# Two token tiles per numerator step in a fused linear-attention and token-mixing kernel

## The chip, the cores and the metric

The kernel runs on one core of a Trainium2 chip, as one launch. The metric is the device time of a launch in microseconds. Five engines run side by side, each through its own list of instructions, in order: TensorE (PE, with its weight loads PEld), VectorE (DVE), ScalarE (ACT), GpSimd (POOL) and SyncE (SP), which here only issues transfers. Semaphores order them where one needs another's result or buffer.

## The reference

Shapes: x 2048 x 512, 32 heads of 16, w1 2048 x 1792, w2 1792 x 2048. All fp32.

```python
q, k, v = split_heads(layernorm(x) @ wqkv)
pq, pk = per_head(q, w_phi), per_head(k, w_phi)
phi_q = concat([softmax(pq), softmax(-pq)])       # over the 16 features, per head
phi_k = concat([softmax(pk), softmax(-pk)])
kv, z = phi_k.T @ v, phi_k.sum(tokens)            # per head
num = phi_q @ kv
den = phi_q @ z + 1e-6
h   = x + (num / den) @ wo
u   = gelu(einsum("sd,sf->df", layernorm(h), w1) + b1)   # across tokens
out = h + (u @ w2 + b2).T
```

## The kernel before

The 2048 tokens are 16 tiles of 128. A matmul of fp32 values is made from three (L62 to L64, `mm3`): operands are split in a high and a low part (`xs`, `whi`/`wlo`, `oh`/`ol`, `hs`) and high x high, low x high, high x low are summed in PSUM.

The launch goes through these stages. Weights are folded and K and V are projected for all tiles, to 113 us; q tiles 0 to 5 are projected among them. A bridge (L419 to L508, to 143.7 us) finishes K and V, makes `zacc` (the sum of phi_k over tokens), spreads it over partitions with a matmul of ones (L487, copied to `zB` at L488), copies wo (`woh`, `wol`) and starts q tiles 6 to 9. The token loop (L630 to L667, 143.7 to 271.5 us) has 19 iterations and is a pipeline over token tiles. The rest of the first matmul of the token mixing runs to 387 us, and the second (`py`, L761) to the end.

From L419 to L669 the orders of PE, DVE, ACT and POOL are written by hand: an instruction stands on its engine where its Python call stands. Only SP's order is a planner's. What an iteration `it` of the loop does, by the names used below:

- q tile: `q_mm` projects a q tile (12 matmuls of 512 columns) into `pu`, a PSUM pool of two buffers. `logit_ops` (L134 to L154) gives DVE three steps per tile: maximum `mx` (L152) and minimum `mn` (L153) per head, and the shift (L145) that writes v-mx into the first half of `eq`. For tiles 0 to 5 the negative logits mn-v are DVE's as well (L150). For tiles 6 to 15 ACT copies v out of PSUM into the second half of `eq` (L147), and later POOL's `negate` (L160) makes mn-v of it in place. `q_exp` (L171, ACT) takes the exponential of both halves; `q_sums` (L216, DVE) sums it per head, once for each half.
- denominator: `ez` (L442, POOL) multiplies by zB, `s_den` (L451 to L457, DVE) sums and divides to a weight `w` for each head and half, and `s_pq` (L460, POOL) scales `eq` by it.
- `s_tr(it)`: PE transposes `eq` in 8 blocks into the PSUM tile `tn` (L525), ACT copies it to `pht` (L527, two copies).
- `s_num(it-1)`: the numerator, 32 small matmuls of 64 rows x 32 columns in the array and 128 tokens (L543), four of a row's blocks and two rows side by side; it uses `tn` too, of which there is one buffer of two banks. ACT copies it to `oh` (L547) and DVE forms `ol` (L552).
- `s_wo(it-2)`: 12 matmuls with wo to `po`; `s_h` (L568, DVE) adds x and stores h. `s_moments`, `s_rstd` and `s_hn` (ACT, POOL) make the layernorm of h and split it to `hs` (L57, L58).
- fills: from iteration 4 (LAG) on, `fill(p)` adds one h tile to the first token-mixing product for a pair p of 128-column blocks of w1 (6 matmuls); p=0 uses the pool `ps_f`, and p=1 `ps_q` once q's tiles are through. `fill_load` loads a w1 part (two token tiles at once), ACT makes `whi` (L604), and `flush` puts the DVE subtraction `wlo` (L596) where it is called.

In iterations 0 to 4 the q tiles 10 to 15 are projected: tile 10 in iteration 0, 11 and 12 in iteration 1, then one in each.

## Time and profile before

| what | us |
|---|---|
| time, median of 3 (lowest, highest) | 534.8 (534.78, 535.04) |
| the profiled execution, its own time | 535.27 |
| its span in the profile | 533.5 |
| token loop, start of first transposes | 143.70 |
| PE busy in 165 to 200 | 32.72 of 35.00 |
| PE busy in 200 to 271.5 | 71.50 of 71.50 |
| PE busy in 271.5 to 387 | 115.50 of 115.50 |
| PE busy in 387 to 533.5 | 141.09 of 146.50 |

The granted clock of TensorE is 0.999. A row of instructions names line, engine, operation, output and inputs, partitions x elements, and how many; then busy time in us, the mean of one in ns, and the idle time of the engine just before them with what ended it. A row of the timeline has start and duration in us first, and in brackets the engine's idle time before it and its releaser. Matmuls overlap: one of 512 columns lasts 390 ns or so but the next starts 227 ns after it.

### The profile page before, as it was taken

Reading aid. Unit: us, or ns where it says so; the run is one execution under the profiler, and the core shown is the slowest. Engines: PE = TensorE matmul, PEld = TensorE weight load, DVE = VectorE, ACT = ScalarE, POOL = GpSimd, SP = SyncE. Lnnn points to the kernel's source line nnn. Section 1 sums busy time; section 2 is a strip of 40 time slices with the busy share of each in tenths; the row PEclk is TensorE's granted clock in tenths of the full one; section 3 lists DMA queues with packets and bytes.
Section 4 is the critical chain, followed back from the end, with each engine's and each line's share of the span. In section 5 each row is a group of like instructions: output and inputs, shape, how many; then the busy total and the mean of one; then the engine's idle time right before and its main releaser. Section 6 shows DMA issues by size and latency. Waiting matters only on the chain.

```text
span 533.5 us, 9887 instructions
## 1 busy us (share of the span) xinstructions
PE 523.4 (98%) x3872; PEld 451.0 (85%) x3872; DVE 382.5 (72%) x680; ACT 277.6 (52%) x470; POOL 228.3 (43%) x180
## 2 busy tenths in 40 slices
PE   8999999999999899999999999999999999999995
PEld 7888888887877777778788888888899999999995
DVE  6893999878798979784235523835768878887784
ACT  6998833525447777666766423525443343343340
POOL 2589699877876978985345000000001101100110
PEclk9999999999999999999999999999999999999999
DMA  8544310022302223333355333533014556535631
GB/s 303 196 124 119 86 35 21 1 62 78 101 1 83 95 81 119 120 109 111 95 159 182 99 100 99 159 111 87 20 41 110 138 149 146 131 120 120 158 78 43
DMA packets 45487, 55.85 MB, mean 105 GB/s; under 512 B 3968, under 2 KB 33024, under 8 KB 45440
## 3 DMA queue, kind: packets, MB, share of 16 engines
q1 hardware_dynamic: 43136, 51.38, 30.3%
q0 software_dynamic: 2016, 3.67, 5.1%
q8 instruction: 30, 0.49, 0.4%
q10 hardware_dynamic: 288, 0.17, 0.1%
q14 instruction: 17, 0.14, 0.1%
HBM read 46.81 MB, written 8.39 MB: 103 GB/s over the span
## 4 chain that ended last, share of the span: by engine, by line
PE 90%; DVE 5%; ACT 3%; issue 1%; POOL 1%; DVEq 0%; ACTq 0%; POOLq 0%
PE py L761 26%; PE pu L62 12%; PE pu L64 12%; PE pu L63 11%; PE po L62 3%; PE pv L63 2%; PE tn L525 2%; PE pv L64 2%; PE pv L62 2%; PE pk_ps L62 2%; PE po L63 2%; PE po L64 2%; PE pk_ps L64 2%; PE pk_ps L63 2%; PE tn L543 2%; PE kvp L207 1%
## 5 line engine op out<-in xcount | busy, mean ns | idle before, releaser
L799 POOL DMA_DIRECT2D out<-ot x14 | 12.5, 1001 | 212.1 <-DVE ot L797 212.1
L761 PE MATMUL py<-uf,whi 128*128 128x256 f32 x560 | 96.2, 283 | 0.0
L62 PE MATMUL pu<-hs,whi 128*128 128x512 f32 x224 | 87.6, 394 | 0.7 <-ACT eq L147 0.7
L57 ACT ACTIVATE whi<-wraw 128x1792 fp32r<-128x1792 f32 x28 | 47.7, 1705 | 77.9 <-PE py L761 62.9
L63 PE MATMUL pu<-hs,whi 128*128 128x512 f32 x224 | 87.2, 389 | 0.0
L64 PE MATMUL pu<-hs,wlo 128*128 128x512 f32 x224 | 87.0, 390 | 0.2 <-DVE wlo L596 0.2
L761 PEld LDWEIGHTS py<-uf,whi 128*128 128x128 f32 x560 | 83.3, 192 | 0.0
L596 DVE TENSOR_TENSOR wlo<-wraw,whi 128x512 fp32r<-128x512 f32 x56 | 46.3, 841 | 45.2 <-ACT whi L604 44.0
L761 PE MATMUL py<-uf,wlo 128*128 128x256 f32 x280 | 69.9, 283 | 0.0
L58 DVE TENSOR_TENSOR wlo<-wraw,whi 128x1792 fp32r<-128x1792 f32 x28 | 56.6, 2023 | 17.8 <-ACT whi L57 17.8
L604 ACT ACTIVATE whi<-wraw 128x512 fp32r<-128x512 f32 x56 | 34.4, 627 | 45.6 <-PE pu L63 41.6
L62 PEld LDWEIGHTS pu<-hs,whi 128*128 128x128 f32 x224 | 42.1, 188 | 9.3 <-ACT eq L147 1.2
L64 PEld LDWEIGHTS pu<-hs,wlo 128*128 128x128 f32 x224 | 42.1, 188 | 9.3 <-DVE wlo L596 0.6
L761 PEld LDWEIGHTS py<-uf,wlo 128*128 128x128 f32 x280 | 49.7, 192 | 0.0
L63 PEld LDWEIGHTS pu<-hs,whi 128*128 128x128 f32 x224 | 42.1, 188 | 8.4
L442 POOL TENSOR_TENSOR ez<-eq,zB 128x1024 f32<-128x1024 f32 x16 | 39.5, 2474 | 0.1
L761 PE MATMUL py<-un,whi 128*128 128x256 f32 x224 | 38.4, 283 | 0.0
L195 POOL TENSOR_TENSOR pk<-pk,sk 128x1024 f32<-128x1024 f32 x16 | 31.1, 1944 | 9.8 <-DVE sk L194 9.0
L460 POOL TENSOR_TENSOR eq<-eq,w 128x1024 f32<-128x1024 f32 x16 | 31.0, 1940 | 5.9 <-DVE w L457 5.9
L527 ACT ACTIVATE pht<-tn 128x512 f32<-128x512 f32 x32 | 17.4, 596 | 30.8 <-PE tn L525 30.8
L761 PEld LDWEIGHTS py<-un,whi 128*128 128x128 f32 x224 | 33.2, 192 | 0.1
L199 POOL TENSOR_TENSOR zacc<-zacc,pk 128x1024 f32<-128x1024 f32 x13 | 31.3, 2406 | 0.6
(165 smaller groups left out, 1192.8 us busy)
## 6 DMA issues: line engine op xcount, KB each, us to landing
wraw<-in_w SPq DMA_DIRECT2D x112, 256.0 KB, 2.9
xraw<-in_xT SPq DMA_DIRECT2D x16, 256.0 KB, 3.1
xh<-in_x SPq DMA_DIRECT2D x16, 256.0 KB, 2.6
h<-in_x SPq DMA_DIRECT2D x16, 256.0 KB, 3.1
out<-h SPq DMA_DIRECT2D x16, 256.0 KB, 2.0
out<-ot POOLq DMA_DIRECT2D x14, 256.0 KB, 4.6
wraw<-in_wT SPq DMA_DIRECT2D x12, 256.0 KB, 5.0
wo<-in_wo SPq DMA_DIRECT2D x4, 256.0 KB, 4.7
```

The costliest lines, as they stand in the source:

```text
L57: nc.scalar.activation(hi, src, AF.Copy)
L58: lo_engine.tensor_sub(lo, src, hi)
L62: nc.tensor.matmul(o, ah, bh, start=first, stop=False)
L63: nc.tensor.matmul(o, ah, bl, start=False, stop=False)
L64: nc.tensor.matmul(o, al, bh, start=False, stop=last)
L195: nc.gpsimd.tensor_mul(heads(PK[t]), heads(PK[t]), sk.unsqueeze(2).to_broadcast([P, 2 * H, DH]))
L199: nc.gpsimd.tensor_add(zacc, zacc, PK[t])
L442: nc.gpsimd.tensor_mul(EZ[t], EQ[t], zB)
L460: nc.gpsimd.tensor_mul(heads(EQ[t]), heads(EQ[t]), W[t].rearrange("p g c h -> p (g c h)").unsqueeze(2).to_broadcast([P, 2 * H, DH]))
L596: LO.append(nc.vector.tensor_sub(wl_, raw, wh_).ins)
L604: nc.scalar.activation(wh_, raw, AF.Copy)
L761: nc.tensor.matmul(o, a[x], b[:, y], start=start and i == 0, stop=stop and i == 2, skip_group_check=True)
```

## The change

- The numerator goes by pairs of token tiles. `pht` holds two tiles, one buffer for all; `s_num(j)` works on tiles 2j and 2j+1 with 32 matmuls of 256 columns, in even iterations only. `oh` and `ol` hold a pair each, one buffer, and are still made tile by tile. `s_wo` and `s_h` stay one tile an iteration, two behind.
- The loop's body is in a new order. The scaling of tile it+1 (`s_pq`) comes first. In even iterations the numerator follows, then the layernorm of h tile it-4 and DVE's `ol`. Then ez, negate, the q tile, the fills, the exponential; after them wo and transposes (transposes first in odd iterations). DVE's logits, sums and denominators come next, then `flush`, then `s_h`.
- The first pair's fills start at iteration 5 and the second's at 6, one of each an iteration, with loads up to one part further ahead. When the loop ends, two and three fills of the pairs are left, for one of each before.
- q's negative logits, tiles 6 to 15: POOL computes mn-mx in place (32 numbers a partition), then subtracts the shifted half of `eq` from it. ACT's copy of v into the second half is still issued, now at the head of `logit_ops` ahead of mx and mn; negate overwrites its result without reading it.

In the changed program, for tiles 6 to 15, DVE's maximum carries a wait for ACT's copy of the same PSUM tile; before, ACT's copy carried a wait for DVE's shift. Ahead of the loop PE's order is the same in both. Counts of instructions are the same but for the numerator (256 small matmuls for 512) and POOL's ten small subtractions.

```diff
-LAG = 4
+LAG = 5
@@ logit_ops
+        if pool:
+            nc.scalar.activation(ev[:, :, 1], v, AF.Copy)
         def shift():
             nc.vector.tensor_sub(ev[:, :, 0], v, mx.unsqueeze(3).to_broadcast([P, NPR, 2, DH]))
             if pool:
-                nc.scalar.activation(ev[:, :, 1], v, AF.Copy)
-                MN.append((ev, mn))
+                MN.append((ev, mx, mn))
@@ negate
-            ev, mn = MN.pop(0)
-            nc.gpsimd.tensor_sub(ev[:, :, 1], mn.unsqueeze(3).to_broadcast([P, NPR, 2, DH]), ev[:, :, 1])
+            ev, mx, mn = MN.pop(0)
+            nc.gpsimd.tensor_sub(mn, mn, mx)
+            nc.gpsimd.tensor_sub(ev[:, :, 1], mn.unsqueeze(3).to_broadcast([P, NPR, 2, DH]), ev[:, :, 0])
@@ s_tr
-        PHT[t] = ak.tile([P, NG, P], F32, name="pht")
+        j, i = divmod(t, 2)
+        if i == 0:
+            PHT[j] = ak.tile([P, NG, 2, P], F32, name="pht", bufs=1)
@@ s_num
-                    nc.tensor.matmul(pn[cols, r, b, :], kvB[rows, b, cols], PHT[t][rows, 4 * b + c, :],
+                    nc.tensor.matmul(pn[cols, r, 2 * b:2 * b + 2, :], kvB[rows, b, cols], PHT[j][rows, 4 * b + c, :, :],
...
+        pv = pn.rearrange("p r (b i) s -> p i r b s", i=2)
+        for i in range(2):
+            nc.scalar.activation(oh[:, i], pv[:, i], AF.Copy)
@@ fill
+        if any(part is WI[p, t - t % 2][1] for part, _, _ in LATER):
             flush()
@@ the loop, as it is after
+    def fills(it):
+        if FN[0] <= it - LAG:
+            fill(0, ps_f)
+        if FN[1] < it - LAG:
+            fill(1, ps_q)
     for it in range(NT + 3):
+        even = it % 2 == 0
+        if 0 <= it + 1 < NT:
+            s_pq(it + 1)
+        if it == 0:
+            s_tr(0)
+            s_kv()
         if it == 1:
             run(q_logits(0))
             q_mm()
+            s_tr(1)
+        if it > 1 and even:
+            if it <= NT:
+                s_num(it // 2 - 1)
+            if it >= 4:
+                s_hn(it - 4)
+        den = s_den(it + 2) if it + 2 < NT else []
+        if it > 1 and even and it <= NT:
+            ol = s_ol(it // 2 - 1)
+            run(ol[:1] + den[:1] + ol[1:])
+            den = den[1:]
+        if it < NT:
+            s_x(it)
+        if it + 3 < NT:
+            s_ez(it + 3)
+        negate()
+        q_mm()
+        fills(it)
+        q_exp(0)
+        logits = q_logits(1)
+        if it >= 3 and even:
+            s_moments(it - 3)
+        if it > 1 and even and it - 2 < NT:
+            s_wo(it - 2)
+        if 1 < it < NT:
+            s_tr(it)
+        if it > 1 and not even and it - 2 < NT:
+            s_wo(it - 2)
+        if it >= 3 and not even:
+            s_moments(it - 3)
+        if it >= 3:
+            s_rstd(it - 3)
+        run(logits + (q_sums(0) if it > 0 else []), den)
+        flush()
+        if 0 <= it - 2 < NT:
+            s_h(it - 2)
         if it > 0:
             negate()
+        if it >= 3 and even:
+            s_hn(it - 3)
         for p in range(2):
-            if it >= LAG - 2 and FL[p] <= FN[p] + 1:
+            if it >= LAG - 2 + p and FL[p] <= FN[p] + 2:
                 fill_load(p)
```

More of the change, by code (lines that the diff above doesn't have):

```diff
@@ L526, in s_tr @@
         for half in range(2):
-            nc.scalar.activation(PHT[t][:, half * 4:half * 4 + 4, :], ptr[:, half], AF.Copy)
+            nc.scalar.activation(PHT[j][:, half * 4:half * 4 + 4, i, :], ptr[:, half], AF.Copy)
     def s_kv():
@@ L534, in s_kv, with s_num @@
         nc.scalar.activation(kvB, pt, AF.Copy)
-    def s_num(t):
-        pn = ps_t.tile([P, 2, 4, P], F32, name="tn")[:, :, 0:2]
+    def s_num(j):
+        pn = ps_t.tile([P, 2, 4, P], F32, name="tn")
         for b in range(2):
@@ L542, in s_num, with s_ol @@
                     rows, cols = slice(64 * r, 64 * r + 64), slice(32 * c, 32 * c + 32)
-                    nc.tensor.matmul(pn[cols, r, b, :], kvB[rows, b, cols], PHT[t][rows, 4 * b + c, :],
+                    nc.tensor.matmul(pn[cols, r, 2 * b:2 * b + 2, :], kvB[rows, b, cols], PHT[j][rows, 4 * b + c, :, :],
                                      start=True, stop=True, skip_group_check=True)
-        oh = ak.tile([P, 2, 2, P], F32R, name="oh")
-        ol = ak.tile([P, 2, 2, P], F32R, name="ol")
-        nc.scalar.activation(oh, pn, AF.Copy)
-        OS[t] = oh, ol, pn
-    def s_ol(t):
-        oh, ol, pn = OS[t]
-        return [lambda: nc.vector.tensor_sub(ol, pn, oh)]
+        oh = ak.tile([P, 2, 2, 2, P], F32R, name="oh", bufs=1)
+        ol = ak.tile([P, 2, 2, 2, P], F32R, name="ol", bufs=1)
+        pv = pn.rearrange("p r (b i) s -> p i r b s", i=2)
+        for i in range(2):
+            nc.scalar.activation(oh[:, i], pv[:, i], AF.Copy)
+        OS[j] = oh, ol, pv
+    def s_ol(j):
+        oh, ol, pv = OS[j]
+        return [lambda i=i: nc.vector.tensor_sub(ol[:, i], pv[:, i], oh[:, i]) for i in range(2)]
     def s_wo(t):
-        oh, ol, _ = OS.pop(t)
+        oh, ol, _ = OS[t // 2]
+        i = t % 2
         PO[t] = po = ps_o.tile([P, D], F32, name="po")
         for j in range(4):
-            mm3(po, oh[:, j // 2, j % 2, :], ol[:, j // 2, j % 2, :], woh[:, j, :], wol[:, j, :], j == 0, j == 3)
+            mm3(po, oh[:, i, j // 2, j % 2, :], ol[:, i, j // 2, j % 2, :], woh[:, j, :], wol[:, j, :], j == 0, j == 3)
     def s_x(t):
@@ L628, in fill @@
                 HN[t][:, 0], HN[t][:, 1], t == 0, t == NT - 1)
-    for it in range(NT + 3):
-        if 0 <= it < NT:
-            s_x(it)
-        if 0 <= it - 1 < NT:
-            s_num(it - 1)
-        if 0 <= it - 3 < NT:
-            s_moments(it - 3)
-        if 0 <= it - 2 < NT:
-            s_wo(it - 2)
+    def fills(it):
[3 more added lines that the diff above has]
+            fill(1, ps_q)
+    for it in range(NT + 3):
+        even = it % 2 == 0
[4 more added lines that the diff above has]
+            s_kv()
         if it == 1:
@@ L641, in block_kernel @@
             q_mm()
-        if 0 <= it < NT:
-            s_tr(it)
-        if it == 0:
-            s_kv()
-        if 0 <= it + 1 < NT:
-            s_pq(it + 1)
-        if 0 <= it - 3 < NT:
-            s_rstd(it - 3)
-        lead(it, 1)
-        den = s_den(it + 2) if it + 2 < NT else []
-        ops = turns((s_ol(it - 1) if 0 <= it - 1 < NT else []) + q_logits(1) + (q_sums(0) if it > 0 else []), den)
-        ops[3:3] = ([lambda: s_h(it - 2)] if 0 <= it - 2 < NT else []) + [flush]
-        run(ops)
+            s_tr(1)
[23 more added lines that the diff above has]
+        if 1 < it < NT:
+            s_tr(it)
+        if it > 1 and not even and it - 2 < NT:
[3 more added lines that the diff above has]
+        if it >= 3:
+            s_rstd(it - 3)
+        run(logits + (q_sums(0) if it > 0 else []), den)
+        flush()
+        if 0 <= it - 2 < NT:
+            s_h(it - 2)
         if it > 0:
             negate()
-        if 0 <= it - 3 < NT:
+        if it >= 3 and even:
             s_hn(it - 3)
-        if FN[0] <= it - LAG:
-            fill(0, ps_f)
-        for _ in range(2):
-            if q["logits"] == NT and FN[1] <= it - LAG:
-                fill(1, ps_q)
         for p in range(2):
-            if it >= LAG - 2 and FL[p] <= FN[p] + 1:
+            if it >= LAG - 2 + p and FL[p] <= FN[p] + 2:
                 fill_load(p)
```

## The prediction

> **What bounds the kernel now.** I read the page's busy time first, then the chain of waits, then what the matmul engine itself waited for.

> ```profile
> PE 523.4 (98%) x3872; PEld 451.0 (85%) x3872; DVE 382.5 (72%) x680; ACT 277.6 (52%) x470; POOL 228.3 (43%) x180
> ...
> PE 90%; DVE 5%; ACT 3%; issue 1%; POOL 1%; DVEq 0%; ACTq 0%; POOLq 0%
> ```

> PE is busy 523.4 of 533.5 us, so a saving must take work or gaps from PE, and any new wait in front of PE is paid in full. These are PE's gaps that the change can reach (us in total, times, longest), and two stretches of the loop (length, then busy PE, PEld, DVE, ACT, POOL):

> ```profile
> PE tn L525 <- POOL hs L58: 1.4, 1, 1.4
> PE pu L62 <- ACT eq L147: 0.7, 1, 0.7
> PE pk_ps L487 <- DVE zacc L480: 0.5, 1, 0.5
> PE pu L64 <- DVE wlo L596: 0.2, 1, 0.2
> ```

> ```profile
> 143.70:150.85 7.15, 7.15 (x72) 5.74 (x66) 6.91 (x15) 4.19 (x7) 4.21 (x4) 1.00 0.26 85
> 200.00:271.50 71.50, 71.50 (x609) 56.66 (x608) 44.69 (x95) 48.55 (x102) 49.96 (x47) 1.00 0.32 104
> ```

> From 200 us on PE never stops and no other engine passes 70%. But at the loop's start DVE has 6.91 of 7.15 us: there is no room for it to wait.

> **The numerator by pairs.** Work per element is unchanged, 8 calls of 256 columns replace 16 of 128.

> ```profile
> L543 PE MATMUL tn<-pht,kvB 64*32 64x128 f32 x512 | 10.7, 275 | 0.0
> L147 ACT ACTIVATE eq<-pu 128x512 f32<-128x512 f32 x10 | 5.9, 595 | 5.8 <-DVE eq L145 5.7
> L160 POOL TENSOR_TENSOR eq<-mn,eq 128x512 f32<-128x512 f32 x10 | 10.9, 1099 | 6.8 <-ACT eq L147 6.8
> ```

> The duration of one matmul overlaps its neighbours, so I take starts. The 32 small matmuls take 597 ns from the first to the next engine operation, the matmul before them holds 318 ns and the one after 337 ns, where 227 is the pitch of an undisturbed 512-column matmul: 597+91+110 = 798 ns a call. A round of 8 starts every 109 to 133 ns. The nearest row for 256 columns of fp32 is L487, whose 512 columns start every 429 ns, so a round takes about 214. One paired call: 91 + 4x214 + about 168 for drain and issue (597 less 4x107) + 110 = 1.23 us against 1.60 for two: 8x0.37 = **-3.0**. Bounds: rounds no longer than now gives -6.4, twice the whole 597 with only the entry and exit saved gives -1.6.

> **The old gaps.** Gaps between starts in 165 to 200 us exceed their pitch by 0.90, 0.33 and 1.53: together **-2.8** if the new order removes all three, 0 if it removes none. The 1.4 is really ol (L552) that frees the transposes' bank late; the numerator now goes an iteration's work earlier, and hn and hs come after it. I take the whole, since my replay of the new order passes these places without them.

> **The negative logits.** POOL's negate now reads the shifted logits; a tiny subtraction is added (128x32; between the 0.19 of L580 and the 1.06 of L160, I take 0.25, ten times, POOL is at 4.21 of 7.15 at worst). ACT's copy L147 stays (10x0.60 on an engine with room, by itself nothing) but is issued ahead of the maximum, and its result is now overwritten unread. Copy and maximum read one bank: before, the copy waited for DVE's shift (the row above says so: 5.7 of its 5.8 us), now in the built order DVE's maximum waits for the copy. That is what decides. Where the copy stands:

> ```profile
> 122.83 0.63 DVE L152 TENSOR_REDUCE mx<-pu 128x32 f32<-128x512 f32 x1
> 123.37 0.68 DVE L153 TENSOR_REDUCE mn<-pu 128x32 f32<-128x512 f32 x1
> 123.96 0.68 DVE L145 TENSOR_TENSOR eq<-pu,mx 128x512 f32<-128x512 f32 x1
> 125.05 1.29 DVE L480 TENSOR_TENSOR zacc<-zacc,pk 128x512 f32<-128x512 f32 x2 [0.41 <-POOL pk L195]
> ```

> ```profile
> 125.81 0.69 ACT L186 ACTIVATE vs<-pv,r 128x512 f32<-128x512 f32 x1 [2.16 <-PE pv L64]
> 126.40 0.59 ACT L147 ACTIVATE eq<-pu 128x512 f32<-128x512 f32 x1
> ```

> ```profile
> 125.89 1.95 PE L487 MATMUL pk_ps<-zacc,ones 128*128 128x512 f32 x4 [0.45 <-DVE zacc L480]
> ```

> A. Bridge. The copy of tile 6 stands on ACT behind vs, which waits for PE's projection of v, and ends at 127.0. Then maximum, minimum, shift (0.55+0.59+0.65) end at 128.85, zacc's first half at 129.5, and PE's L487, now at 125.89, starts at 129.6: **+3.7** (to 4.4 if POOL's negate, also freed by the shift, is in zacc's way). Queued behind zacc on DVE are wol and all else; tiles 7 and 8 lose nothing more, as DVE idles 3.4 us before kvS. The loop starts at 147.4 for 143.70.

> B. Start of the loop.

> ```profile
> 146.07 1.16 ACT L171 ACTIVATE eq<-eq,r 128x1024 f32<-128x1024 f32 x1
> 147.31 0.60 ACT L147 ACTIVATE eq<-pu 128x512 f32<-128x512 f32 x1
> 150.14 0.60 ACT L147 ACTIVATE eq<-pu 128x512 f32<-128x512 f32 x1 [1.04 <-DVE eq L145]
> ```

> The copy of tile 9 stands behind pht, kvB and the exponential and ends 4.2 after the loop's start: 151.6. Maximum, minimum and shift with the sums between them take 3.1 (144.18 to 147.20 now): 154.7. PE's q tile 11 needs that bank (two buffers), and PE is through with tile 10 at 151.3: **+3.4**. Then the copy of tile 11 stands behind the exponential of tile 9, that behind POOL's negate, that behind w: w(2) 155.75, scaling L460 1.94, ez 2.40, negate 0.25+1.06, exponential 1.05, copy 0.60, logits 3.1 come to 166.2. PE has q 11, transposes, q 12 and a numerator (2.73+0.88+2.73+1.23) and is free at 162.3: **+4.0** (3 to 4.6). Iterations 2 to 4 have nothing left that PE waits for.

> C. First fills.

> ```profile
> 193.16 2.09 DVE L596 TENSOR_TENSOR wlo<-wraw,whi 128x512 fp32r<-128x512 f32 x1
> ```

> ```profile
> 192.31 2.39 POOL L442 TENSOR_TENSOR ez<-eq,zB 128x1024 f32<-128x1024 f32 x1
> ```

> Fills now stand right behind the q tile, and wlo goes last on DVE, after sums and den. The first fill of iteration 5 needs a wlo that DVE reaches at 188.1 and ends between 188.7 and 189.5; PE, free at 187.0, waits for its third part 1.7 to 2.5, **+2.2**. The second pair's first fill, an iteration later, has the same wlo wait and a wo that needs h, now behind wlo: **+2.0** (1 to 3). The rows show why I don't take the lower ends: wlo is 0.69 alone, 2.09 when ez started first, ending 0.55 after it.

> [...]

> From iteration 7 PE has 14.3 less 0.37 for two iterations and DVE, POOL and ACT have room (the second stretch above). The loads move with the fills: SP's queue gains no transfer and no wait that reaches ACT's whi, since four w1 buffers are loaded before the first fill; a load late by its 2.9 us would add to C what exceeds the lead. LAG 5 leaves five fills instead of two behind the loop: the same matmuls, covered by others there.

> **Sum.** +3.7+3.4+4.0+2.2+2.0 = 15.3 new, -2.8 old, -3.0 numerator: +9.6. Against the profiled execution's 535.27 (span 533.5 and 1.77 around it): 544.85, span 543.1. That execution lies 0.47 over the median, so the median goes 534.8 to **544.4**. With every term at its low end (numerator -6.4, 3.0 for the second part of B, 1.7 and 1.0 in C) it is 538.4; with every one at its high end (4.4 in A, 4.6 in B, 2.5 and 3.0 in C, numerator -1.6, old gaps kept) 551.1.

> **Rivals.** 1. *The copy holds nothing up*, as ACT runs ahead. Then A and B fall to about 2 us in all, C stays near 0.3, and the time is 534.8+2.3-5.7 = **531.4**. It decides below 5.7 us of new waits. For it: ACT is busy 52%. Against: it is busy behind vs and the exponential just where the copies stand.

> [...]

> 2. *Only the bridge pays*: PE waits at L487, and POOL, ACT and DVE use these 3.7 us to catch up, so that B and C nearly vanish (2.2 left): 534.8+3.7+2.2-5.7 = **535.0**. Against: tile 9's copy hangs on PE's transposes, which move too.

> 3. *DVE stays behind*: after B, wlo and h last on DVE, each blocked by POOL for up to 1.4 us, keep costing in iterations 7 to 10: 4 to 6 more, **549**. For it: from 165 to 200 us DVE works 29.0 of 35 already. Against: logits end with iteration 4.

> **How the numbers follow.** Forecast 0.72, rival 1 0.06, rival 2 0.10, rival 3 0.12. A measurement tells about 0.2% (1.07 us) from no change. Rival 1 is faster; rival 2 lies at no change, 0.02 of it faster, 0.03 same, 0.05 slower; all else is slower: 0.08, 0.03, 0.89. The range 537.5 to 550 leaves out rivals 1 and 2 and the tips of the rest.

> **What would show it.** PE idle before L487 of about 4.2, released by zacc; DVE idle before the maximum released by ACT's copy, near 125 and in the loop's first two iterations; PE idle of 3 to 4 at the q tiles 11 and 13; PE's L64 waiting for wlo at the first fills; the numerator's PE row at 256 matmuls with starts 214 ns a round. If DVE's maximum does not wait for ACT, or PE's gaps sum to less than 6 us between 120 and 205, the forecast is wrong.

## The result, and the profile after

| kernel | median us | lowest, highest | ratio to before (95% interval) |
|---|---|---|---|
| before | 534.92 | 534.78, 535.26 | |
| after | 550.62 | 549.80, 551.40 | 1.0292 (1.0277 to 1.0307) |

The change makes the kernel slower by 15.7 us where +9.6 was forecast; 550.62 lies just above the range's 550. The direction was right and so were the first places where PE stands still; the size was not. The profiled execution of after took 550.16 us with a span of 548.4.

The page of after, busy time and the chain of waits:

```profile
PE 525.6 (96%) x3616; PEld 451.8 (82%) x3616; DVE 383.9 (70%) x680; ACT 276.9 (51%) x470; POOL 233.5 (43%) x190
...
PE 81%; POOL 9%; DVE 4%; ACT 3%; issue 2%; DMA 1%; DVEq 0%; POOLq 0%; ACTq 0%
```

POOL's share of the chain went from 1% to 9%. The chain now runs through POOL's negate, the exponential and the copy at 158 to 165 us, but that is the small part: 39 of the 45 us that POOL has on it lie between 210 and 255 us, where PE waits for almost nothing. So this share isn't what the change costs. What PE waited for in after (total, times, longest), and the groups that the change touched:

```profile
PE pu L62 <- DVE eq L147: 5.4, 2, 3.1
PE pu L64 <- DVE wlo L604: 4.9, 2, 2.8
PE pk_ps L489 <- DVE zacc L482: 4.2, 1, 4.2
...
PE pu L63 <- POOL hs L58: 0.6, 1, 0.6
```

```profile
L153 DVE TENSOR_REDUCE mx<-pu 128x32 f32<-128x512 f32 x16 | 11.0, 690 | 22.3 <-ACT eq L144 19.7 <-POOL eq L462 2.2 <-PE pu L64 0.3
...
L144 ACT ACTIVATE eq<-pu 128x512 f32<-128x512 f32 x10 | 5.9, 591 | 0.1
...
L161 POOL TENSOR_TENSOR mn<-mn,mx 128x32 f32<-128x32 f32 x10 | 2.5, 252 | 4.4 <-DVE mn L154 4.4
```

Before, the copy waited 5.7 us for DVE's shift. Now DVE's maximum idles 19.7 us for the copy. The copy itself costs what it did, and POOL's new subtraction the 0.25 us taken. Four of the maximum's waits, on DVE:

```profile
126.37 0.69 DVE L153 TENSOR_REDUCE mx<-pu 128x32 f32<-128x512 f32 x1 [4.12 <-ACT eq L144]
...
153.38 0.69 DVE L153 TENSOR_REDUCE mx<-pu 128x32 f32<-128x512 f32 x1 [3.49 <-ACT eq L144]
...
164.91 0.69 DVE L153 TENSOR_REDUCE mx<-pu 128x32 f32<-128x512 f32 x1 [5.59 <-ACT eq L144]
...
195.28 0.69 DVE L153 TENSOR_REDUCE mx<-pu 128x32 f32<-128x512 f32 x1 [1.99 <-ACT eq L144]
```

They are tiles 6, 9, 11 and 15. The first three answer to A and B of the prediction; the last, in iteration 5, was not foreseen. And PE at the places where it then stood still:

```profile
129.00 3.75 PE L489 MATMUL pk_ps<-zacc,ones 128*128 128x512 f32 x4 [4.21 <-DVE zacc L482]
...
156.55 0.50 PE L62 MATMUL pu<-wqh,xs 128*128 128x512 f32 x1 [3.12 <-DVE eq L147]
...
168.08 0.63 PE L62 MATMUL pu<-wqh,xs 128*128 128x512 f32 x1 [2.27 <-DVE eq L147]
...
203.49 0.50 PE L64 MATMUL pu<-hs,wlo 128*128 128x512 f32 x1 [2.83 <-DVE wlo L604]
```

Look at the first row's duration: four matmuls took 3.75 us that took 1.95 before. The stretches of after around these gaps (length, busy PE, PEld, DVE, ACT, POOL, and then PE's granted clock, transfer share, GB/s) say why:

```profile
129.00:134.00 5.00, 5.00 (x8) 2.59 (x9) 3.72 (x5) 1.81 (x3) 1.31 (x2) 0.50 0.00 0
134.00:153.00 19.00, 19.00 (x207) 15.51 (x206) 8.97 (x19) 6.46 (x11) 15.32 (x10) 1.00 0.35 113
...
158.00:160.60 2.60, 2.60 (x8) 1.87 (x7) 1.32 (x3) 0.00 (x0) 2.60 (x2) 0.51 0.00 0
...
168.00:171.70 3.70, 3.62 (x9) 2.84 (x10) 3.63 (x9) 0.52 (x2) 1.50 (x1) 0.54 0.00 0
```

After each of three gaps TensorE works at about half clock: 0.50, 0.51 and 0.54 are granted in the rows of 5.00, 2.60 and 3.70 us. Busy time hides it: in the first of these rows PE is busy for 5.00 of 5.00 us. The prediction's sum had no term for that.

### The profile page after: what moved, and what is told of

Same layout as the page of the kernel before. It is cut to its first block, busy times and chain, and to the rows that moved or that the text cites. A ratio compares the mean times of both kernels' runs of the same rounds, so it can differ in the third digit from the quotient of the medians.

```text
span 548.4 us, 9397 instructions
## 1 busy us (share of the span) xinstructions
PE 525.6 (96%) x3616; PEld 451.8 (82%) x3616; DVE 383.9 (70%) x680; ACT 276.9 (51%) x470; POOL 233.5 (43%) x190
## 4 chain that ended last, share of the span: by engine, by line
PE 81%; POOL 9%; DVE 4%; ACT 3%; issue 2%; DMA 1%; DVEq 0%; POOLq 0%; ACTq 0%
PE py L791 25%; PE pu L62 11%; PE pu L64 10%; PE pu L63 10%; POOL ez L444 3%; PE pv L63 3%; PE pv L64 3%; PE pv L62 3%; POOL eq L462 2%; PE pk_ps L62 2%; PE pk_ps L64 2%; PE pk_ps L63 2%; PE kvp L209 2%; POOL hs L58 1%; PE po L64 1%
## 5 line engine op out<-in xcount | busy, mean ns | idle before, releaser
L64 PE MATMUL pu<-hs,wlo 128*128 128x512 f32 x224 | 87.3, 390 | 4.9 <-DVE wlo L604 4.9
L62 PE MATMUL pu<-hs,whi 128*128 128x512 f32 x224 | 87.4, 395 | 0.0
L604 DVE TENSOR_TENSOR wlo<-wraw,whi 128x512 fp32r<-128x512 f32 x56 | 49.6, 889 | 51.9 <-ACT whi L612 50.8
L58 DVE TENSOR_TENSOR wlo<-wraw,whi 128x1792 fp32r<-128x1792 f32 x28 | 56.6, 2022 | 14.7 <-ACT whi L57 14.5
L64 PEld LDWEIGHTS pu<-hs,wlo 128*128 128x128 f32 x224 | 42.0, 188 | 14.6 <-DVE wlo L604 5.8
L62 PEld LDWEIGHTS pu<-hs,whi 128*128 128x128 f32 x224 | 42.1, 188 | 10.7 <-issue 2.5
L62 PE MATMUL pu<-wqh,xs 128*128 128x512 f32 x64 | 28.4, 443 | 5.4 <-DVE eq L147 5.4
```

The source lines that it names most:

```text
L58: lo_engine.tensor_sub(lo, src, hi)
L62: nc.tensor.matmul(o, ah, bh, start=first, stop=False)
L64: nc.tensor.matmul(o, al, bh, start=False, stop=last)
L604: LO.append(nc.vector.tensor_sub(wl_, raw, wh_).ins)
```

## The experiments

All ratios are to the kernel before in runs on the same chip; its medians there were 535.01 (e1 to e4), 535.19 (e5 to e8) and 534.74 (e9 to e12).

| run | median us | ratio (95% interval) |
|---|---|---|
| e1, after without the copy | 533.96 | 0.9982 (0.9973 to 0.9991) |
| e2, copy behind the shift | 536.74 | 1.0032 (1.0020 to 1.0045) |
| e3, before with the copy first | 556.19 | 1.0399 (1.0375 to 1.0423) |
| e4, PE kept busy in three gaps | 549.68 | 1.0270 (1.0254 to 1.0285) |
| e5, before with shifted negation, no copy | 534.56 | 0.9986 (0.9977 to 0.9995) |
| e6, e4 and one more gap | 547.58 | 1.0229 (1.0215 to 1.0243) |
| e7, e1 with wlo and h early | 538.80 | 1.0065 (1.0052 to 1.0079) |
| e8, e1 with the numerator in halves | 534.41 | 0.9986 (0.9977 to 0.9995) |
| e9, copy for tiles 6 to 8 alone | 539.45 | 1.0083 (1.0069 to 1.0097) |
| e10, copy for tiles 9 to 15 alone | 545.62 | 1.0213 (1.0188 to 1.0237) |
| e11, no copy for tiles 14, 15 | 547.75 | 1.0243 (1.0223 to 1.0264) |
| e12, e1 with h ahead of wlo | 534.52 | 0.9991 (0.9982 to 0.9999) |

**e1, the copy taken out of after.**

```diff
-        if pool:
-            nc.scalar.activation(ev[:, :, 1], v, AF.Copy)
```

> The changed kernel without ACT's copy of v (its result is unread). Theory A (the maximum's wait for that copy, and TensorE at half clock behind each long gap, make nearly all of the excess): the gap before the matmul of ones is back to about 0.5 us, PE has no gap over 1.5 us ahead of the q tiles 11 and 13, granted clock 1.00; left are the numerator (-3.0), the old gaps (-2.8), the first fills' waits for wlo (measured 2.5 and 3.3 in the changed kernel) and some 1.5 in iterations 7 to 12: 534.9 - 5.8 + 5.8 + 1.5 = 536.4, 535 to 538.5. Theory B (the new order of the loop does the harm, the copy is one wait among many): over 545.

533.96 us, clock 0.999. What PE waited for in e1:

```profile
PE tn L546 <- ACT pht L529: 1.2, 2, 1.0
PE pu L63 <- POOL hs L58: 1.2, 2, 0.6
PE pu L64 <- DVE wlo L602: 1.1, 1, 1.1
...
PE pk_ps L487 <- DVE zacc L480: 0.9, 2, 0.5
```

No wait for the shift is left, and the gap before the matmul of ones is back to 0.5 us. The copy where it stands costs 16.7 us (550.62 less 533.96); all else that the change does gains about 1 us. The figure expected was too slow by 2.4, since the first fills' waits, carried over from after at 5.8, fell to 1.1: they too hung on the copy.

**e2, the copy behind the shift.** Its result is as unread as before.

```diff
             if pool:
+                nc.scalar.activation(ev[:, :, 1], v, AF.Copy)
                 MN.append((ev, mx, mn))
```

> The changed kernel with the unread copy put back behind DVE's shift, where it stood before. Theory A (place): as without the copy, 536.4, at most 1 us more since POOL's negate now waits for 0.6 us of copy that lies 1 us ahead of it. Theory C (the copy's own 0.60 us on ACT, ten times, delay the exponentials): 541 to 551.

536.74, which is 2.8 more than e1 and 13.9 less than after. Place is most of it, but a copy that nobody reads is not free behind the shift either: PE waits 1.9 us for it, 1.7 at one q tile, because the copy holds the PSUM buffer that the q tile is to have. Theory C's range is missed, and the 1 us allowed over e1 is too little.

**e3, before with only the copy moved ahead of the maximum.**

```diff
+        if pool:
+            nc.scalar.activation(ev[:, :, 1], v, AF.Copy)
         def shift():
...
             if pool:
-                nc.scalar.activation(ev[:, :, 1], v, AF.Copy)
```

> The kernel before, with nothing changed but the place of ACT's copy: ahead of the maximum. Theory A: gap before the matmul of ones 4.2 us and TensorE at half clock behind it (+3.8 and +2.5), then a gap of 3 or more at a q tile in iterations 0 to 2 with half clock behind it (+5), perhaps a second (+3): 545 to 551. Theory B (the copy hurts only in the new order): at most 537.

556.19: the move alone does more harm in the old order than the whole change in the new. PE's waits in e3:

```profile
PE pu L62 <- DVE eq L147: 6.5, 2, 4.0
PE tn L526 <- DVE ol L553: 5.4, 4, 2.1
PE pk_ps L488 <- DVE zacc L481: 4.8, 1, 4.8
```

The time lies 5.2 us above the range of theory A, and the second row, which theory A did not have, is 5.4: with DVE late, ol frees the transposes' bank late four times. That the row makes the excess is read from these two numbers; no run takes that wait out. The new order, with ol ahead of the logits, doesn't have that wait.

**e4 and e6, PE kept busy in the gaps.** The added matmuls write PSUM that the next real matmul starts anew; all waits stay. e4 fills three gaps, e6 also the one before the second pair's first fill.

```diff
+    def spin(o, n):
+        for i in range(n):
+            nc.tensor.matmul(o, X[NT - 1][:, 0, i % KD, :], wqh[:, i % KD, :], start=True, stop=True)
...
+        if g == 0:
+            spin(pz.rearrange("p g s -> p (g s)"), 17)      # ahead of the matmul of ones
...
+            spin(ps_o.tile([P, D], F32, name="po"), 12)     # ahead of q tile 11
...
+            spin(ps_o.tile([P, D], F32, name="po"), 9)      # ahead of q tile 13
...
+        if t == 0 and p == 1:                               # e6 alone, in fill
+            for i in range(14):
+                nc.tensor.matmul(PU[p][0], woh[:, 0, 0:P], woh[:, i % KD, :], start=True, stop=True)
```

> The changed kernel with 17 matmuls of no use ahead of the matmul of ones, 12 ahead of q tile 11 and 9 ahead of q tile 13, in the gaps in which PE idles; all waits stay as they are. Theory A: TensorE's clock stays at 1.00 and what follows runs at its full pitch: 2.5 us less at the bridge, 1 to 3.5 less in iterations 1 and 2 (a later wait may take some of it up): 544.5 to 547. Rival (the long matmuls behind the gaps have another cause, or the time is set by DVE and POOL, not by PE's pace): 549.5 to 551.

> The run with PE kept busy, and 14 more matmuls of no use ahead of the second pair's first fill, where PE idled 3.7 us and fell to half clock. Theory A (half clock costs what it slows): its last cold stretch, 201 to 206 us, goes, 1.7 us less than that run: 548; the clock is then at 1.00 throughout, and 550.6 less this time is all that half clock cost the changed kernel, the rest is waits. Rival (iterations 6 on are set by DVE and POOL, so PE's pace there is worth nothing): 549.5.

e4 took 549.68, 0.9 less than after: the rival's time at first sight. The trace says otherwise. The loop starts at 147.56 for after's 149.33 and the first fill stands at 186.73 for 189.96, so 3.2 us are gained by then; but the second pair's first fill then waits longer, 3.5 us for 2.8, and the granted clock falls there: it is 0.90 from 175 to 205 us. PE's waits in e4, and on DVE what the fill waited for:

```profile
PE pu L64 <- DVE wlo L610: 5.2, 2, 3.5
PE pu L62 <- DVE eq L147: 2.0, 2, 1.6
```

```profile
192.20 0.69 DVE L153 TENSOR_REDUCE mx<-pu 128x32 f32<-128x512 f32 x1 [2.54 <-ACT eq L144]
...
197.33 3.13 DVE L610 TENSOR_TENSOR wlo<-wraw,whi 128x512 fp32r<-128x512 f32 x2
```

e6 fills that gap as well, and the granted clock of its whole execution is 1.000. Two stretches of e6, columns as above:

```profile
129.00:134.00 5.00, 4.46 (x15) 2.74 (x16) 3.93 (x6) 2.23 (x3) 2.49 (x2) 1.00 0.01 3
134.00:205.00 71.00, 66.93 (x516) 52.49 (x515) 52.47 (x107) 35.55 (x64) 57.06 (x47) 1.00 0.21 67
```

547.58 us. So the half clock cost after 550.62 - 547.58 = 3.0 us net, and the waits alone 547.58 - 534.92 = 12.7. (The two ran in different rounds; by the ratios of the tables it is 3.4 and 12.3.) Counted from the pitches of after the half clock slowed PE by 5.8: 2.5 at the bridge, then 1.6 (six q matmuls at 427 and not 227 ns, and the transposes behind them), then 1.7. About half of that is time that PE would else have waited for DVE: from the numerator to q tile 13 PE takes 3.4 us in after and 5.0 in e6, and the second pair's first fill waits 3.0 us in after and 3.7 in e6, the added matmuls not counted.

**e5, the negation from the shifted logits alone, on the kernel before, no copy.**

```diff
-                nc.scalar.activation(ev[:, :, 1], v, AF.Copy)
-                MN.append((ev, mn))
+                MN.append((ev, mx, mn))
...
-            nc.gpsimd.tensor_sub(ev[:, :, 1], mn.unsqueeze(3).to_broadcast([P, NPR, 2, DH]), ev[:, :, 1])
+            nc.gpsimd.tensor_sub(mn, mn, mx)
+            nc.gpsimd.tensor_sub(ev[:, :, 1], mn.unsqueeze(3).to_broadcast([P, NPR, 2, DH]), ev[:, :, 0])
```

> The kernel before with its negative logits taken from the shifted ones and no copy at all: part d of the change alone, as its name says. Theory A (only the copy's place is harmful): nothing waits in its place; what it can gain is the 0.7 us at the first fill that was put down to the copy, and 0.60 us of ACT ten times that nobody waited for: 533.8 to 535.2. Rival (POOL, with 0.25 us more a tile, becomes late for the exponentials): 536 to 540.

534.56, 0.14% faster, within what was expected. Without the copy this part of the change does no harm, and POOL carries the ten small subtractions without a loss.

**e7 and e12, the order of wlo and h on DVE in e1.** e7 puts both back among the sums, e12 only h ahead of wlo from iteration 7 on.

```diff
-        run(logits + (q_sums(0) if it > 0 else []), den)
-        flush()
-        if 0 <= it - 2 < NT:
-            s_h(it - 2)
+        ops = turns(logits + (q_sums(0) if it > 0 else []), den)
+        ops[3:3] = ([lambda: s_h(it - 2)] if 0 <= it - 2 < NT else []) + [flush]
+        run(ops)
```

```diff
-        flush()
+        if it < 7:
+            flush()
         if 0 <= it - 2 < NT:
             s_h(it - 2)
+        flush()
```

> The changed kernel without the copy, and with wlo and h back among DVE's sums, where they stood before, h first. Theory A (wlo last on DVE costs the first fill its wait): the 1.1 us at the first fill goes, h earlier helps wo: 532.5 to 533.3 against 534.0 without it. Rival (den, now behind wlo, makes w and POOL's scaling late, so transposes wait): 534 to 537.

> The changed kernel without the copy, with h ahead of wlo on DVE from iteration 7 on (both still behind the sums). Theory A (hn and hs come late through h: PE waits 1.2 us for hs and 1.0 for a numerator whose copies stand behind hn): h earlier by 0.6 to 1.9 saves part of it: 532.8 to 533.7. Rival (wlo later, or the waits are POOL's and ACT's queues): 533.9 to 535.

e7 took 538.80, which is 4.8 us more than e1 and above the ranges of both theories, so wlo and h at the end of DVE's turn belong to the gain, though not for the rival's reason alone. On DVE in e7:

```profile
166.31 0.68 DVE L152 TENSOR_REDUCE mn<-pu 128x32 f32<-128x512 f32 x1
169.60 0.69 DVE L574 SCALAR_TENSOR_TENSOR h<-po,h 128x512 f32<-128x512 f32 x1 [2.61 <-PE po L64]
...
170.32 0.68 DVE L145 TENSOR_TENSOR eq<-pu,mx 128x512 f32<-128x512 f32 x1
```

h stands ahead of the shift and waits 2.6 us for wo, which the new order has behind the q tile on PE; the shift, and the q tile that needs its bank, wait behind h. PE's waits for the shift are 1.3 us in all, though; wo's wait for ol is another 1.3 and the fills' wait for wlo rises from 1.1 to 1.8. What the rest of the 4.8 is stays open. e12 gains nothing over e1 (534.52 against 533.96), as its rival had it: its waits for hs and pht are the same 1.2 and 1.2.

**e8, the paired call with its columns in halves.**

```diff
+        for i in range(2):
...
-                    nc.tensor.matmul(pn[cols, r, 2 * b:2 * b + 2, :], kvB[rows, b, cols], PHT[j][rows, 4 * b + c, :, :],
+                        nc.tensor.matmul(pn[cols, r, 2 * b + i, :], kvB[rows, b, cols], PHT[j][rows, 4 * b + c, i, :],
```

> The changed kernel without the copy, with the two tiles of a numerator as 64 small matmuls of 128 columns, back to back, instead of 32 of 256: the calls are still paired. Theory A (what the pairing saves is one entry, one drain and one exit of the array's small tiles, the columns cost the same): 8 rounds of 109 to 133 and one drain of 246 are 1.03 us, as the paired call's 1.02 now: no change, 533.6 to 534.4. Rival (longer matmuls save issue): 8 times 0.2 to 0.4, 535.5 to 537.

534.41, for e1's 533.96; the numerator's matmuls keep PE busy for 9.2 us in all with 64 short ones a call (e8), for 8.8 with 32 long ones (after). The pairing's gain is one entry and one exit of the small tiles instead of two; by the starts in before they take 91 and 110 ns over the pitch of 227. Longer matmuls add next to nothing.

**e9, e10, e11, the copy for some tiles only.**

```diff
-        if pool:
+        if copy:                      # e9: tiles under 9; e10: from 9 on; e11: under 14
             nc.scalar.activation(ev[:, :, 1], v, AF.Copy)
```

> The changed kernel with the unread copy for tiles 6 to 8 alone, whose logits stand in the bridge. Theory A (the bridge's gap and the half clock behind it are paid on their own): 534.0 without any copy, +3.8 and +2.5, less what later waits give back (at most the 2.3 that PE waits for the first fill and a numerator): 538 to 540.5; gap before the matmul of ones 4.2. Rival (the other engines catch up while PE waits, the bridge pays little): 534.5 to 537.

> The changed kernel with the unread copy for tiles 9 to 15 alone, whose logits stand in the loop. Theory A: 550.6 less the bridge's 3.8 and 2.5: 544.3, 542.5 to 546; gaps at the q tiles 11 and 13 as with all copies, with half clock behind them. Rival (the loop's gaps are there only because the bridge comes late): 534 to 538.

> The changed kernel with the unread copy for all of 6 to 15 but tiles 14 and 15. Theory A (the second pair's first fill waits so long because the maximum of tile 15 stood 2.0 us behind its copy and wlo stands behind its sums): that fill's gap goes from 2.8 to under 1: 547 to 549. Rival (it waits because GpSimd holds up wlo, 3.0 us for two): 550 to 551.5.

The three times are 539.45, 545.62 and 547.75, all within theory A's ranges. The four runs of e10 lie far apart, though, from 544.62 to 548.03 us, and the longer ones have the lower granted clock (0.993 down to 0.990); what makes them differ was not shown. PE's waits in e9 (first row) and in e11 (second fence):

```profile
PE pk_ps L489 <- DVE zacc L482: 4.2, 1, 4.2
```

```profile
PE pu L62 <- DVE eq L147: 5.4, 2, 3.1
PE pk_ps L489 <- DVE zacc L482: 4.5, 2, 4.2
...
PE pu L64 <- DVE wlo L604: 1.1, 1, 1.1
```

The bridge's share is 5.5 us over e1, the loop's 11.7, together 17.2 for the 16.7 of all copies: the two places add up, as far as the spread of e10 lets one say. Without the copies of tiles 14 and 15 the fills' wait for wlo falls from 4.9 to 1.1, all of it the first pair's, and the time by 2.9. That settles what held up the second pair's first fill: the rival, by which GpSimd holds up wlo whatever the copies do, had 550 us or more.

## Why the prediction was right and wrong

**Right.** That the copy, read by nobody, would hold up the maximum from its new place, and that this decides the sign (e1 against after, e3 by itself). A: a gap of 4.21 where 4.2 was forecast (the shift's end there adds to 128.79, not 128.85, which changes nothing). B: with PE kept at full clock, q tiles 11 and 13 start at 154.77 and 166.33 in e4, forecast 154.7 and 166.2; in after itself the gaps are only 3.1 and 2.3 us, since half clock took the rest. The first fill's gap came to 2.2 in after (2.47 us between starts, less the pitch of 0.23), as forecast, but that is partly luck: at full clock, in e6, it is 1.8. The paired numerator: 1.02 us between the first small matmul and the next operation, the 4x214+168 of the sum.

**Wrong, a term that was left out: the clock.** A and B were costed as idle time alone, "+3.7", "+3.4", "+4.0". This is the first step that failed. Behind each of these gaps PE ran at 0.50 to 0.54 of its clock, which cost 3.0 us net (after against e6), half of the 6.1 by which the forecast fell short. The trace of before could not show it, since no gap there after the start is longer than 1.4 us and the granted clock is 1.00 from 7 to 532 us.

Full clock came back in after at 134.16, 161.47 and 171.71 us, each time after 3.41 us in which PE was busy for all of them. The length of a gap alone doesn't tell what follows it: half clock came with gaps of 4.2, 3.1 and 2.3 us, but not with the one of 2.8; the last section has the busy time around each.

**Wrong, a term that was too small: C.** "The second pair's first fill, an iteration later, has the same wlo wait" was put at +2.0, 3 at most. From start to start and less the pitch it measured 3.0 in after, where the half clock had delayed PE, and 3.7 in e4 and e6, where it had not. The second step that failed is "Iterations 2 to 4 have nothing left that PE waits for", taken to mean that DVE is free of the copy by then, and with it "logits end with iteration 4". PE indeed waits for nothing in iterations 2 to 4. But in the new order tile 15's logits stand in iteration 5, behind their copy and ahead of the second pair's wlo: DVE waits for the copy 0.5 us at tile 14 and 2.0 at tile 15, and its wlo then meets POOL's scaling, 3.02 us for two, where the median of all is 0.69 for one. e11 shows this: without these two copies that fill doesn't wait.

**A term that was missing, small.** Matmul starts in iterations 7 to 12 exceed their pitch by 1.2 us in all, mostly at a fill that waits for hs; the forecast had "PE has 14.3 less 0.37 for two iterations" and room on all other engines. With 1.7 for the second pair's first fill and 3.0 for the clock this makes 5.9 of the 6.1 by which the forecast fell short. The sum is no better than the runs: two smaller misses are left out of it and nearly cancel, both at the full clock of e6. The bridge, from PE's last matmul ahead of the gap to the loop, takes 4.4 us more there than in before, for 3.7, and the first fill's gap is 0.4 less than forecast.

**Rivals.** 1, the copy holds nothing up: refuted by after, and e1 is what that world costs, 533.96 where 531.4 was worked out; waits in e1's loop that replace the old gaps (for pht, hs and wlo) sum to 3.5 us. 2, only the bridge pays: refuted, e9 pays 5.5 us for it, e10 11.7 for the loop without it. 3, DVE stays behind: it does so for one iteration longer than the forecast had it, at tile 15, and not beyond 205 us, where PE is busy 69.2 of 70 us. Its time, 549, is nearer to the measured one than the forecast's, but not for its reason, waits in iterations 7 to 10; and h, which it counts with wlo as blocked by POOL, took 0.68 to 0.69 us all sixteen times in after.

## What to carry to other kernels

An instruction whose result nobody reads can still hold up others, as this copy did for 16.7 us: look at what it reads, which buffer it holds and what waits for that, and take it out when its reader goes. Before an instruction is moved ahead of another engine's on the same PSUM bank, look at what stands ahead of it on its own engine, for all that is now in front of the other: here the maximum idled 19.7 us for the copy. Gaps of 4.21, 3.12 and 2.27 us in front of TensorE came here with a granted clock of 0.50 to 0.54 in the work behind them, one of 2.83 with the full clock: when a change can open such gaps, look at the clock behind them, and then ask how much of the loss another engine's lateness would have taken anyway.

e1 is faster than before by 0.18% (0.09 to 0.27%), the lowest ratio of these kernels; e5, e8 and e12 can't be told from it by their intervals.

## What was unexpected of the hardware

From its first fall, at 127.34 us, the granted clock of after stays at half for 6.83 us, at full for 23.89, at half for 3.41, at full for 6.83 and at half for 3.41: 2, 7, 1, 2 and 1 times 3.41, to 0.03 us. Some stretches of that length, laid off from these changes, columns as above:

```profile
123.92:127.34 3.42, 0.86 (x4) 0.38 (x2) 0.97 (x2) 1.18 (x2) 0.44 (x1) 1.00 0.01 2
...
151.23:154.64 3.41, 2.19 (x10) 1.46 (x8) 1.26 (x2) 2.72 (x5) 0.09 (x1) 1.00 0.00 0
154.64:158.06 3.42, 1.51 (x7) 1.26 (x8) 3.32 (x10) 0.00 (x0) 0.46 (x1) 1.00 0.00 0
158.06:161.47 3.41, 3.41 (x12) 2.72 (x11) 1.26 (x3) 0.00 (x0) 3.41 (x2) 0.50 0.00 0
164.88:168.30 3.42, 1.15 (x33) 0.55 (x20) 3.35 (x7) 2.38 (x4) 0.00 (x0) 1.00 0.00 0
...
199.02:202.43 3.41, 1.64 (x8) 1.00 (x6) 3.38 (x7) 3.16 (x5) 3.19 (x4) 1.00 0.16 53
202.43:205.84 3.41, 2.35 (x10) 1.94 (x11) 3.41 (x6) 1.31 (x4) 3.41 (x3) 1.00 0.63 184
```

The clock fell at the end of the first, the third and the fifth, with PE busy for 0.86, 1.51 and 1.15 us, and not after the second and the last two, with 2.19, 1.64 and 2.35. The gap of 2.83 us, 200.66 to 203.49, lies in both of the last two. So in after the half clock went with PE's busy time in these stretches, and not with the length of a gap; what sets the clock, no run here takes apart. Whether the spread of e10's times comes from it stays open, since only one of its runs has a trace.
